# Plain loads and computed row numbers at the start of a Fourier mixing and hard-swish kernel

## The chip, the cores and the metric

The kernel runs on one core of a Trainium2 chip. The metric is device microseconds of one execution. Before the change the median of 3 runs is 1931.91 us (1931.62 to 1932.03).

The core has TensorE (PE, with its weight loads as PEld), VectorE (DVE), ScalarE (ACT), GpSimd (POOL) and SyncE (SP). DMAs are issued from SP, ACT and POOL and carried by 16 DMA engines. Each engine works through its own instructions in order and waits on semaphores.

## The reference

```python
# x: (8, 3008, 256) f32; w_in: (256, 2048); w_out: (2048, 256), given as 8-byte floats
X = np.fft.fft(x, axis=1)
X = np.fft.fft(X, axis=2).real          # mixing over sequence and features
h = X.reshape(24064, 256) @ w_in
out = (h * np.clip(h + 3.0, 0.0, 6.0) / 6.0) @ w_out
```

## The kernel before, in words

The Fourier transform over 3008 = 47 x 64 positions is done in two stages, stage 1 over 47 and stage 2 over 64, and symmetric halves of it are added ahead of the products ("folds"): a row group of x (64 + 48 partitions, 4 positions of 256 values in each) is added to its partner group, which lies mirrored in memory. The transform over the 256 features is multiplied into `w_in` once (`fold_w_in`), with a table `C`. Then come 24064 rows of an MLP in chunks: products `u` and `v` (L541), an activation on DVE and ACT, and the products with `w_out` (L616 and L636).

The batches are worked in four pairs. Only the start for the first batch is touched by the change; it is written out by hand, engine by engine, in the order of the program (`manual_schedule`).

- `load_half` fetches one group m of the first batch with two indirect DMAs from POOL: the forward rows and the partner rows (`gather`, L174). The row numbers stand in `IX`, cast by DVE (L875) from the table `FI` that SP loads first. Groups come in the order 3, 0, 1, 2 (`ORDER`).
- `fold_half` (L204 to L233) adds partners on DVE, `stage1_early` (L320 to L364) does the products on PE, copies them to `z` (L350 to L352) and stores `z` to memory (`zd`, L364). `load_g_half` (L432) reads it back, transposed, for stage 2 (`stage2_half`, L451; `spread_by_pe`, L472).
- The weights arrive as 8-byte floats, in 16 pieces of 512 KB (`load_w`, L740 and L744, POOL). A piece is turned into 4-byte floats by `exponent_a` (bytes, ACT, L760), `exponent_b` (PE, L774, with the matrix `E`), `exponent_c` (ACT, L777), `mantissa` (DVE, L785, L786) and `join` (DVE, L794, or L800 for `w_out`). A `w_in` piece is then multiplied by `C` (`fold_w_in`, PE, L829) and copied to `W1` (L832). The last row of each block of `W1` is wanted as a column `WN`: `send_wn` (L817) sends it by a small DMA from SP; for the first two blocks a small product (L946) makes it.
- `keep_awake` (L853) multiplies zeros on PE where there is nothing else to do.
- `see` (L903) is a small copy on POOL that holds back the loads behind it until its operand is there.

Piece 0 of `w_in` holds the column blocks f = 0 and 1, piece 1 the blocks 8 and 9. One MLP step with index fc uses the blocks fc and fc + 8. In the program's order both pieces are loaded ahead of all gathers, their exponents are done ahead of stage 1, and both are folded between stage 1 and stage 2:

```python
    for j in range(2):
        load_w(j)
    ...
    for k, m in enumerate(ORDER):
        load_half(hb, m)
```

A DMA takes one of 8 semaphore lanes for each kind of issuer; the ninth waits for the first to land.

Of the kernel before, what the change touches and what calls it, by code (L numbers as in the profile page):

```python
# [58 lines left out]
def kernel(  # L59
# [113 lines left out]
    def gather(xr, i, nr=PX, skip=0):  # L173
        nc.gpsimd.indirect_dma_start(  # L174
            out=xr[0:nr].rearrange("p n d -> p (n d)"), out_offset=None, in_=x_r,
            in_offset=bass.IndirectOffsetOnAxis(ap=IX[0:nr, i:i + 1], axis=0), element_offset=skip,
        )

    class Half:
# [6 lines left out]
    def take_half(hb, m, pool=xpool, tag="x"):  # L186
        hb.x[m], hb.xr[m] = x_tile(pool, tag), x_tile(pool, tag)

    def load_half(hb, m):
        start = hb.b * N1 * N2 * D  # L190
        gather(hb.x[m], NP * NXC + m, P, start + D)
        gather(hb.xr[m], m, P, start)

    def load_zero(o, hb, queue):
        queue.dma_start(out=o, in_=x_pn[hb.b * N1:(hb.b + 1) * N1, 0, :])

    def zero_slot(hb):
        return hb.x[NM - 1][PB:PB + N1, XC - 1, :]
# [332 lines left out]
    def mlp1_products(ch, fc, between=None):  # L531
        of, nq, q = ch.ck % 2 * TB, ch.nq, ch.pr.q[ch.ck // 2]
        u = ps_h.tile([P, 2, TB], F32, tag="uv", name="u")
        v = ps_h.tile([P, 2, TB], F32, tag="uv", name="v")
        for blk, ps in ((0, u), (1, v)):
            if blk and between:
                between()
            r = slice(0, P - blk)
            for i in range(2):
                f = fc + i * NF  # L540
                nc.tensor.matmul(ps[:, i, 0:nq], W1[r, blk, f * P:(f + 1) * P], q[r, blk, of:of + nq],  # L541
                                 start=True, stop=True)
        return u, v
# [182 lines left out]
    STRAIGHT = (0, 1, 8, 9, 14, 15)  # L726
    NEXT = {4: 10, 5: 11, 6: 12, 7: 13, 8: 14, 9: 15}

    def in_column(n, i):
        return (2 * n + i * NF) * P  # L730

    def load_w(j):
        kind, n, i = PIECES[j]

        pool, tag, bufs = (wpool, "st", 2) if j in STRAIGHT else (spool, "t", None) if j in (2, 3) else (xpool, "x", None)
        st = pool.tile([P, 2 * WB], I32, tag=tag, bufs=bufs, name="st")
        o = st[:].bitcast(moe_w_in.dtype)
        if kind == "in":
            cs = slice(in_column(n, i), in_column(n, i) + WB // 2)
            nc.gpsimd.dma_start(out=o.rearrange("p (c j) -> p c j", c=2),  # L740
                                in_=moe_w_in[:, cs].rearrange("(c p) f -> p c f", p=P))
# [11 lines left out]

    def exponent_a(j):
        top = raw[j][:].bitcast(I16).rearrange("p (n four) -> p n four", four=4)[:, :, 3]
        for i in range(2):
            low = PM[j % len(PM)][:, i].bitcast(U8).rearrange("p (n two) -> p n two", two=2)[:, :, 0]
            nc.scalar.activation(low, top, AF.Identity, bias=bias[:, i:i + 1], scale=(1 - 2 * i) / 16.0)  # L760

    def exponent_b(j, own=False):
        pm = [PM[j % len(PM)][:, i].bitcast(F16) for i in range(2)]
        if starting[0] and not own:
            exs[j] = ps_h.tile([P, WB], F32, tag="uv", name="ex")[:]
        elif own:
            exs[j] = ps_d.tile([P, WB], F32, tag="d", name="ex")[:]
        elif j % 2 == 0:
            exs[j] = bank([P, WB], "ex")[:]
        else:  # L770

            exs[j] = spare[1 if j % 4 == 1 else 0][:].rearrange("p i n -> p (i n)")
        for i in range(2):
            nc.tensor.matmul(exs[j], E[:, i], pm[i], start=(i == 0), stop=(i == 1))  # L774
# [41 lines left out]
    def send_wn(f):  # L816
        nc.sync.dma_start(out=WN[:, f:f + 1], in_=W1[P - 1:P, 1, f * P:(f + 1) * P])  # L817

    def fold_w_in(j):

        _, n, k = PIECES[j]
        nb = WB // 2
        cs = slice(in_column(n, k), in_column(n, k) + nb)
        wi = w.pop(PIECES[j]).rearrange("p (i f) -> p i f", i=2)

        ps = bank([P, 2, nb], "wps") if starting[0] else spare[k]
        for blk in range(2):
            for i in range(2):
                nc.tensor.matmul(ps[:, blk], C[:, i, blk * P:(blk + 1) * P], wi[:, i], start=(i == 0), stop=(i == 1))  # L829
        fs = range(cs.start // P, cs.stop // P)  # L830
        if starting[0]:
            nc.vector.tensor_copy(W1[:, :, cs], ps[:])  # L832
            return wi, fs
# [15 lines left out]
    def keep_awake(n, ps=None):  # L849
        if ps is None:  # L850
            ps = ps_d.tile([P, 2 * TB], F32, tag="d", name="awake")
        for i in range(n):
            nc.tensor.matmul(ps[:], ones[:], Z[:], start=True, stop=True)  # L853
# [1 line left out]
    Z = spool.tile([P, 2 * TB], F32, tag="s", name="Z")  # L855
    nc.vector.memset(Z[:], 0.0)
    nc.vector.memset(ones[:], 1.0)
    keep_awake(6)
    hb = halves[0]
    nc.sync.dma_start(out=FI[:], in_=c_stage1[:, 14 * PB:])  # L860
    nc.sync.dma_start(out=F[:], in_=c_stage1[:, 0:7 * PB])
    first_slot = qpool.tile([P, 2 * TB], F32, tag="qn", name="first_slot")
    load_zero(first_slot[PB:PB + N1, 0:D], hb, nc.sync)
# [6 lines left out]
    def clear_bytes(j):  # L870
        nc.vector.memset(PM[j][:].rearrange("p i n -> p (i n)").bitcast(I32), 0x64006400)

    clear_bytes(0)
    nc.vector.memset(half[:], 0.5)
    nc.vector.tensor_copy(IX[:], FI[:, 0:NIX])  # L875
    clear_bytes(1)
    clear_bytes(2)
    for k, m in enumerate(ORDER):
        take_half(hb, m, *((xpool, "x"), (xpool, "x"), (qpool, "q"), (apool, "a"))[k])

    def clear_table(b):
        r = slice((1 - b) * N2, (2 - b) * N2)
        t = T[r, b].rearrange("p g a k n -> p g (a k n)")
        nc.scalar.copy(t, Z[r].unsqueeze(1).to_broadcast([N2, NG, 2 * TB]))

    clear_table(0)

    def head(j):
        exponent_a(j)
# [13 lines left out]
        nc.gpsimd.tensor_copy(seen[:], x)  # L903

    for j in range(2):
        load_w(j)
    nc.gpsimd.affine_select(E[:, 0], ones[:], pattern=[[-1, P]], compare_op=AL.is_equal, fill=0.0, base=0,
                            channel_multiplier=1)  # L910
    nc.scalar.mul(E[:, 1], E[:, 0], -1.0)
# [6 lines left out]
    for j in range(2):  # L918
        exponent_a(j)
        mantissa(j)  # L920
    exponent_b(0)
    keep_awake(2)
    exponent_b(1, own=True)
    nc.scalar.copy(zero_slot(hb), first_slot[PB:PB + N1, 0:D])
    exponent_c(0)
    exponent_c(1)
    clear_table(1)
    keep_awake(4, bank([P, 2 * TB], "awake"))
# [12 lines left out]
    join(1)  # L941
    folds = [fold_w_in(j) for j in range(2)]
    wn = ps_d.tile([P, 2], F32, tag="d", name="wn")
    for c, (wi, fs) in enumerate(folds):
        for i in range(2):
            nc.tensor.matmul(wn[:, c:c + 1], wi[:, i, 0:P], C[:, i, D - 1:D], start=(i == 0), stop=(i == 1))  # L946
    nc.vector.tensor_copy(WN[:, 0:NFC:NF], wn[:])
    for wi, fs in folds:
        send_wn(fs[1])
# [7 lines left out]
    mantissa(2)  # L957
    exponent_a(2)
    exponent_b(2)
    mantissa(3)  # L960
    exponent_a(3)
    exponent_c(2)
# [197 lines left out]
def _tables(B, S, D):  # L1160
# [41 lines left out]
    f = np.concatenate([f0.reshape(128, -1), f1.reshape(128, -1), row.reshape(128, -1), forward, sign], axis=1)  # L1202

    k = k1[:, None] + N1 * np.arange(N2)
    n2 = np.arange(N2 // 2) + 1
# [42 lines left out]
```

## Time and profile before

| | |
|---|---|
| median of 3 runs | 1931.91 us |
| profiled execution | 1931.28 us, its span 1929.6 us |
| granted TensorE clock | 0.999 |
| PE busy | 1916.0 us, 99% |
| DVE, ACT, POOL busy | 1426.9, 679.6, 1443.3 us |
| bytes by DMA | 99.02 MB, 51 GB/s over the span |
| DMA rate in the first 32 us | 275 GB/s |

Times in the rows are in microseconds from the start of the span. A row of the timeline gives start, duration, engine (a name with q is the engine's DMA queue), line, operation, destination and source with their shapes, a count, and in brackets the idle time of the engine before it with what ended it. A row of busy times by stretch gives the stretch, its length, the busy time and the instruction count of each engine, the granted clock, the share of time that the DMA engines were busy, and GB/s.

### The profile page before, as it was taken

Reading aid. Unit: us, or ns where it says so; the run is one execution under the profiler, and the core shown is the slowest. Engines: PE = TensorE matmul, PEld = TensorE weight load, DVE = VectorE, ACT = ScalarE, POOL = GpSimd, SP = SyncE. Lnnn points to the kernel's source line nnn. Section 1 sums busy time; section 2 is a strip of 40 time slices with the busy share of each in tenths; the row PEclk is TensorE's granted clock in tenths of the full one; section 3 lists DMA queues with packets and bytes.
Section 4 is the critical chain, followed back from the end, with each engine's and each line's share of the span. In section 5 each row is a group of like instructions: output and inputs, shape, how many; then the busy total and the mean of one; then the engine's idle time right before and its main releaser. Section 6 shows DMA issues by size and latency. Waiting matters only on the chain.

```text
span 1929.6 us, 28216 instructions
## 1 busy us (share of the span) xinstructions
PE 1916.0 (99%) x9362; PEld 1652.4 (86%) x9362; DVE 1426.9 (74%) x2762; ACT 679.6 (35%) x1164; POOL 1443.3 (75%) x1652
## 2 busy tenths in 40 slices
PE   9999999999999999999999999999999999999998
PEld 5688888888988888888898888888899888888887
DVE  7867776777777777777787777777778777777777
ACT  6533333333333333333333333333333333333332
POOL 4697888896688778787678877878666667666765
PEclk9999999999999999999999999999999999999999
DMA  8432232211112222121111221221110101101000
GB/s 285 123 88 51 62 81 65 64 44 40 30 39 71 55 52 55 45 56 37 27 38 50 51 55 44 53 53 50 36 28 20 28 17 27 34 11 28 19 21 20
DMA packets 154473, 99.02 MB, mean 51 GB/s; under 512 B 121941, under 2 KB 135998, under 8 KB 154326
## 3 DMA queue, kind: packets, MB, share of 16 engines
q1 hardware_dynamic: 141926, 57.38, 12.3%
q0 software_dynamic: 11456, 39.56, 7.0%
q8 instruction: 74, 1.21, 0.3%
q14 instruction: 73, 0.60, 0.1%
q10 hardware_dynamic: 944, 0.26, 0.1%
HBM read 59.84 MB, written 37.32 MB: 50 GB/s over the span
## 4 chain that ended last, share of the span: by engine, by line
PE 96%; DVE 2%; ACT 1%; DMA 0%; issue 0%; SPq 0%; DVEq 0%; ACTq 0%; POOLq 0%
PE acc L636 56%; PE v L541 16%; PE u L541 16%; PE ps L490 2%; PE acc L616 1%; PE ps L279 1%; DVE a L592 1%; PE spare L829 1%; DVE s L550 1%; DVE o L697 0%; ACT t L589 0%; PE ps L451 0%; DMA st<-in_moe_w_in_dram 0%; PE awake L853 0%; DVE u L573 0%
## 5 line engine op out<-in xcount | busy, mean ns | idle before, releaser
L606 POOL TENSOR_TENSOR c<-a 128x512 f32<-128x512 f32 (+1 forms) x375 | 469.1, 1251 | 360.2 <-PE acc L636 309.6
L636 PE MATMUL acc<-c,G 128*128 128x256 f32 (+1 forms) x3008 | 697.2, 375 | 0.0
L589 ACT ACTIVATE t<-u,half 128x512 f32<-128x512 f32 (+1 forms) x384 | 260.6, 679 | 1142.6 <-DVE u L560 1063.3
L636 PEld LDWEIGHTS acc<-c,G 128*128 128x128 f32 x3008 | 565.2, 190 | 71.6 <-POOL c L606 0.4
L550 DVE SCALAR_TENSOR_TENSOR s<-qn,WN,u 128x256 f32<-128x256 f32 (+1 forms) x768 | 330.5, 472 | 341.0 <-PE u L541 338.1
L636 PE MATMUL acc<-a,G 128*128 128x256 f32 (+1 forms) x2256 | 541.6, 375 | 0.0
L636 PEld LDWEIGHTS acc<-a,G 128*128 128x128 f32 x2256 | 421.0, 189 | 73.6 <-issue 20.2
L541 PE MATMUL v<-q,W 127*128 127x256 f32 (+1 forms) x1536 | 389.3, 375 | 2.3 <-DVE a L592 2.3
L541 PE MATMUL u<-q,W 128*128 128x256 f32 (+1 forms) x1536 | 388.0, 375 | 0.2 <-ACT q L454 0.2
L592 DVE SCALAR_TENSOR_TENSOR a<-t,u 128x512 f32<-128x512 f32 (+2 forms) x448 | 264.1, 601 | 101.0 <-ACT t L589 97.3
L541 PEld LDWEIGHTS v<-q,W 127*128 127x128 f32 x1536 | 288.0, 190 | 42.9 <-DVE a L592 3.1
L541 PEld LDWEIGHTS u<-q,W 128*128 128x128 f32 x1536 | 285.8, 190 | 37.4 <-issue 2.4
L606 POOL TENSOR_TENSOR c<-a,c 128x256 f32<-128x256 f32 (+1 forms) x375 | 268.6, 716 | 29.4
L606 POOL TENSOR_TENSOR c<-c,a 128x256 f32<-128x256 f32 (+1 forms) x375 | 268.3, 716 | 29.4
L560 DVE TENSOR_TENSOR u<-s,v 128x512 f32<-128x512 f32 x352 | 245.0, 696 | 37.4 <-DVE s L550 0.9
L592 DVE SCALAR_TENSOR_TENSOR a<-t,v 128x512 f32<-128x512 f32 (+1 forms) x480 | 263.6, 565 | 0.3
L589 ACT ACTIVATE t<-v,half 128x512 f32<-128x512 f32 (+1 forms) x384 | 260.5, 678 | 0.6 <-issue 0.4
L562 DVE TENSOR_TENSOR v<-v,s 128x512 f32<-128x512 f32 x352 | 243.9, 693 | 0.0
L606 POOL TENSOR_TENSOR r<-w,e 128x256 f32<-128x256 f32 (+1 forms) x92 | 88.7, 985 | 3.6
L646 ACT ACTIVATE e<-acc 128x512 f32<-128x512 f32 (+2 forms) x184 | 83.3, 544 | 0.0
L697 DVE STREAM_TRANSPOSE o<-r 128x256 f32<-128x256 f32 (+1 forms) x192 | 72.5, 415 | 0.2
L606 POOL TENSOR_TENSOR w<-w,e 128x512 f32<-128x512 f32 (+1 forms) x46 | 57.5, 1251 | 3.6
(139 smaller groups left out, 775.9 us busy)
## 6 DMA issues: line engine op xcount, KB each, us to landing
out_dram<-o SPq DMA_DIRECT2D x744, 32.0 KB
g<-zd SPq DMA_DIRECT2D x42, 256.0 KB
zd<-z SPq DMA_DIRECT2D x48, 192.0 KB
xt<-in_x_dram POOLq DMA_DIRECT2D x21, 256.0 KB
st<-in_moe_w_in_dram POOLq DMA_DIRECT2D x8, 512.0 KB
st<-in_moe_w_out_dram POOLq DMA_DIRECT2D x8, 512.0 KB
qn<-qd SPq DMA_DIRECT2D x16, 256.0 KB
xt<-in_x_dram POOLq DMA_DIRECT2D x17, 192.0 KB
```

The costliest lines, as they stand in the source:

```text
L279: nc.tensor.matmul(ps[b][h * PB:(h + 1) * PB, 0:n], F[rows(b), 0:PB], y[rows(b), 2 * h:2 * h + n], start=True, stop=not last, skip_group_c ...
L490: nc.tensor.matmul(ps[:, blk, u * P:n].rearrange("p (b k) -> p b k", b=2), g[:, kk, blk * (P + 1):blk * (P + 1) + P], T[:, :, gr, blk, kk, ...
L541: nc.tensor.matmul(ps[:, i, 0:nq], W1[r, blk, f * P:(f + 1) * P], q[r, blk, of:of + nq], start=True, stop=True)
L550: nc.vector.scalar_tensor_tensor(s[:, i, 0:nq], qn[:, of:of + nq], WN[:, f:f + 1], u[:, i, 0:nq], op0=AL.mult, op1=AL.add)
L560: nc.vector.tensor_tensor(u[:], s[:], v[:], op=AL.add)
L562: nc.vector.tensor_tensor(v[:], v[:], s[:], op=AL.subtract)
L589: nc.scalar.activation(t, h, AF.Relu, bias=half[:], scale=scale)
L592: nc.vector.scalar_tensor_tensor(dst, t, 1.0, h, op0=AL.min, op1=AL.mult)
L606: (eng or nc.gpsimd).tensor_tensor(out, in0, in1, op=AL.add)
L636: nc.tensor.matmul(ch.acc[i // 2][:, i % 2, 0:ch.n], G[:, i, fc, :], mv, start=(fc == 0 and i % 2 == 0), stop=(fc == NF - 1), skip_group_c ...
L646: nc.scalar.mul(ch.e[:, k:i + 1, 0:ch.n], ch.acc[i // 2][:, 0:i + 1 - k, 0:ch.n], 1.0 / WS)
L697: nc.vector.transpose(o[:, 0:n // DH, h], ch.r[:, m, h, 0:n].rearrange("p (j i) -> p j i", i=DH))
```

## The change

Row numbers are made on POOL by two iotas and a maximum, into a new table `IT`; the table of the other groups is stored as integers in `FI` and used without a cast. The forward rows of the first batch come by plain loads: the first half of the first group from ACT's queue, everything else from SP's, the zero column directly to its place (48 rows in place of 47). Only partners are gathered, 112 rows in place of 128. The first weight piece is loaded ahead of the last gather, the second behind it; the first two pieces hold other columns than before: piece 0 the blocks 0 and 8, piece 1 the blocks 1 and 9, each loaded by two DMAs of 128 columns. Preparation of piece 0 moves between the groups of stage 1, that of piece 1 behind stage 1, interleaved with pieces 2 and 3; `WN` of the first two pieces comes by `send_wn`. Two PSUM tiles at the first steps change pools, and wake-up products become fewer.

```diff
-    IX = consts.tile([P, NIX], I32, name="IX")
+    IX = FI[:, 0:NIX].bitcast(I32)
+    IT = consts.tile([P, NM], I32, name="IT")
...
+    def load_rows(hb, m, h, queue):
+        c, nr = m + h * NM, (PB, N1 + 1)[h]
+        n = XC - (c == NXC - 1)
+        queue.dma_start(out=hb.x[m][h * PB:h * PB + nr, 0:n, :], in_=x_pn[0:nr, c * XC + 1:c * XC + 1 + n, :])
...
-        v = ps_h.tile([P, 2, TB], F32, tag="uv", name="v")
+        pool, tag = (ps_d, "d") if ch.first and fc == 1 else (ps_h, "uv")
+        v = pool.tile([P, 2, TB], F32, tag=tag, name="v")
...
+    def in_columns(n, i):
+        if n == 0:
+            return [(i + h * NF) * P for h in range(2)]
+        return [(2 * n + i * NF + h) * P for h in range(2)]
...
-    keep_awake(6)
+    keep_awake(7)
...
+    for h in range(2):
+        nc.gpsimd.iota(IT[h * PB:(h + 1) * PB], [[-1, NM]], base=2 * NXC * N1 - 1 - h * NM,
+                       channel_multiplier=-2 * NXC)
+    nc.gpsimd.tensor_single_scalar(IT[:], IT[:], 0, op=AL.max)
+    load_rows(hb, ORDER[0], 0, nc.scalar)
+    load_rows(hb, ORDER[0], 1, nc.sync)
+    load_zero(zero_slot(hb), hb, nc.sync)
+    for m in ORDER[1:]:
+        for h in range(2):
+            load_rows(hb, m, h, nc.sync)
+        if m == ORDER[1]:
+            nc.sync.dma_start(out=F[:], in_=c_stage1[:, 0:7 * PB])
     nc.sync.dma_start(out=FI[:], in_=c_stage1[:, 14 * PB:])
-    nc.sync.dma_start(out=F[:], in_=c_stage1[:, 0:7 * PB])
...
-    for j in range(2):
-        load_w(j)
...
     for k, m in enumerate(ORDER):
-        load_half(hb, m)
+        if k == NM - 1:
+            load_w(0)
+        gather(hb.xr[m], m)
...
+    load_w(1)
     nc.gpsimd.dma_start(out=C[:], in_=c_dim.rearrange("(h p) d -> p h d", p=P))
...
     for k, m in enumerate(ORDER):
         if m in SPLIT:
+            mantissa(0)
             for j in range(2):
                 fold_columns(hb, m, j, nc.vector)
             join(0)
...
         stage1_early(hb, m)
+        if k == 0:
+            exponent_a(0)
+        elif k == 2:
+            exponent_b(0)
+            exponent_c(0)
...
+    mantissa(1)
+    fold_w_in(0)
+    exponent_a(1)
+    exponent_b(1)
+    keep_awake(1)
+    exponent_a(2, (0,))
+    exponent_c(1)
+    exponent_a(2, (1,))
+    mantissa(2)
     join(1)
-    folds = [fold_w_in(j) for j in range(2)]
...
-    see(W1[:, 0, NF * P:NF * P + 1])
+    see(w[PIECES[1]][:, 0:1])
...
     exponent_b(2)
+    exponent_a(3, (0,))
+    exponent_c(2)
+    exponent_a(3, (1,))
     mantissa(3)
...
+    fold_w_in(1)
     exponent_b(3)
-    keep_awake(1)
     join(2)
     tail(3)
     stage2_half(hb, 0)
```

More of the change, by code (lines that the diff above doesn't have):

```diff
@@ L738, in load_w @@
         if kind == "in":
-            cs = slice(in_column(n, i), in_column(n, i) + WB // 2)
-            nc.gpsimd.dma_start(out=o.rearrange("p (c j) -> p c j", c=2),
-                                in_=moe_w_in[:, cs].rearrange("(c p) f -> p c f", p=P))
+            c0, c1 = in_columns(n, i)
+            for h, cs in enumerate((slice(c0, c1 + P),) if n else (slice(c0, c0 + P), slice(c1, c1 + P))):
+                nf = cs.stop - cs.start
+                nc.gpsimd.dma_start(out=o.rearrange("p (c j) -> p c j", c=2)[:, :, h * P:h * P + nf],
+                                    in_=moe_w_in[:, cs].rearrange("(c p) f -> p c f", p=P))
         else:
@@ L746, in load_w, with exponent_a @@
         raw[j] = st
-    def exponent_a(j):
+    def exponent_a(j, signs=range(2)):
         top = raw[j][:].bitcast(I16).rearrange("p (n four) -> p n four", four=4)[:, :, 3]
-        for i in range(2):
+        for i in signs:
             low = PM[j % len(PM)][:, i].bitcast(U8).rearrange("p (n two) -> p n two", two=2)[:, :, 0]
@@ L763, in exponent_b @@
         pm = [PM[j % len(PM)][:, i].bitcast(F16) for i in range(2)]
-        if starting[0] and not own:
+        if (starting[0] or j == 4) and not own:
             exs[j] = ps_h.tile([P, WB], F32, tag="uv", name="ex")[:]
@@ L829, in fold_w_in @@
                 nc.tensor.matmul(ps[:, blk], C[:, i, blk * P:(blk + 1) * P], wi[:, i], start=(i == 0), stop=(i == 1))
[L830 to L833, printed above, removed]
+        fs = (c0 // P, c1 // P)
+        if n == 0:
+            o = W1[:].rearrange("p b (h f) -> p b h f", h=2)[:, :, :, c0:c0 + P]
+            nc.vector.tensor_copy(o, ps[:].rearrange("p b (h f) -> p b h f", h=2))
+            for f in fs:
+                send_wn(f)
+            return
         nc.scalar.copy(W1[:, :, cs], ps[:])
@@ L871, in clear_bytes @@
         nc.vector.memset(PM[j][:].rearrange("p i n -> p (i n)").bitcast(I32), 0x64006400)
-    clear_bytes(0)
     nc.vector.memset(half[:], 0.5)
[L875 to L879, printed above, removed]
+    for j in range(3):
+        clear_bytes(j)
     def clear_table(b):
@@ L917 @@
         load_w(j)
[L918 to L926, printed above, removed]
+    clear_table(0)
+    nc.scalar.mul(E[:, 1], E[:, 0], -1.0)
     clear_table(1)
-    keep_awake(4, bank([P, 2 * TB], "awake"))
     for k, m in enumerate(ORDER):
         if m in SPLIT:
+            mantissa(0)
             for j in range(2):
@@ L1201, in _tables @@
     sign = 1.0 - 2.0 * (np.arange(128)[:, None] % 2)
-    f = np.concatenate([f0.reshape(128, -1), f1.reshape(128, -1), row.reshape(128, -1), forward, sign], axis=1)
+    index = np.concatenate([row.reshape(128, -1), forward], axis=1).astype(np.int32).view(np.float32)
+    f = np.concatenate([f0.reshape(128, -1), f1.reshape(128, -1), index, sign], axis=1)
     k = k1[:, None] + N1 * np.arange(N2)
```

33 lines of the change are left out of this document (10 added, 23 removed).

## The prediction, as recorded before the run

> **What bounds the kernel now.** I read the page first, then busy time by stretch, then the first 45 us instruction by instruction, then the chain that ended last over the same stretch.
>
> ```profile
> PE 1916.0 (99%) x9362; PEld 1652.4 (86%) x9362; DVE 1426.9 (74%) x2762; ACT 679.6 (35%) x1164; POOL 1443.3 (75%) x1652
> ```
> ```profile
> 0.00:32.00 32.00, 29.15 (x239) 17.87 (x240) 20.56 (x53) 20.65 (x34) 17.81 (x28) 1.00 0.84 275
> 32.00:110.00 78.00, 76.44 (x302) 50.20 (x301) 66.22 (x121) 44.80 (x76) 46.03 (x61) 1.00 0.52 160
> 110.00:300.00 190.00, 190.00 (x912) 162.80 (x911) 135.67 (x244) 67.95 (x118) 159.54 (x179) 1.00 0.27 66
> ```
>
> The columns of the second fence are the stretch, its length, busy time of PE, PEld, DVE, ACT and POOL, the granted clock, the DMA share and GB/s. PE is full from 110 us on (190.00 of 190.00). Both kernels issue the same instructions in the same order from the first MLP chunks on, so whatever the change does is a shift of the point at which PE becomes continuously busy. The chain shows where that is:
>
> ```profile
> 32.24 0.95 DVE s L550 x2
> ...
> 40.40 0.60 DVE wi L794
> 41.04 1.99 PE spare L829 x8
> ```
>
> From 41.04 on the chain is PE work almost without a break. From 32.24 to 41.04 it is DVE work in a row, in an order that the change leaves as it is. So the question is when the first `s` on DVE starts: 32.24 now. The start before it, in order of time (start, duration, engine, line, operation, idle before):
>
> ```profile
> 0.41 0.12 POOL L1232 MEMSET const-uint8-127<- 128x1 uint8 x1
> 0.82 0.41 SPq L860 DMA_DIRECT2D FI<-in_c_stage_dram  x1
> 1.29 0.42 SPq L861 DMA_DIRECT2D F<-in_c_stage_dram  x1
> 1.37 1.67 POOL L740 DMA_DIRECT2D st<-in_moe_w_in_dram  x2 [0.84 <-POOLq L1232]
> 1.68 6.89 PE L853 MATMUL awake<-Z,ones 128*128 128x512 f32 x12 [1.68 <-DVE ones L857]
> 2.11 2.75 ACT L884 COPY T<-Z 64x3072 f32<-64x3072 f32 x1
> 2.76 0.29 DVE L875 CAST IX<-FI 128x36 int32<-128x36 f32 x1 [0.57 <-DMA FI<-in_c_stage_dram]
> 3.14 0.30 POOL L909 TENSOR_SCALAR_AFFINE_SELECT E<-ones 128x128 f16<-128x128 f32 x1
> 3.64 1.07 POOL L174 DMA_INDIRECT xt<-in_x_dram,IX  x1 [0.19 <-DVE PM L871]
> 5.02 0.97 POOL L174 DMA_INDIRECT xt<-in_x_dram,IX  x1 [0.31 <-issue]
> 7.82 0.43 DVE L785 TENSOR_SCALAR top<-st 128x512 int32<-128x512 int32 x1 [3.81 <-DMA st<-in_moe_w_in_dram]
> 8.29 0.69 DVE L786 SCALAR_TENSOR_TENSOR top<-st,top 128x512 f32<-128x512 uint32 x1
> 11.66 0.56 DVE L215 TENSOR_TENSOR xt<-xt 111x381 f32<-111x381 f32 x1 [1.48 <-DMA xt<-in_x_dram,IX]
> 12.57 0.94 POOL L174 DMA_INDIRECT xt<-in_x_dram,IX  x1 [0.30 <-issue]
> 15.43 0.69 DVE L215 TENSOR_TENSOR xt<-xt 111x508 f32<-111x508 f32 x1
> 16.77 0.69 DVE L215 TENSOR_TENSOR xt<-xt 111x508 f32<-111x508 f32 x1
> 19.30 0.17 DVE L226 TENSOR_TENSOR y<-xt 111x8 f32<-111x8 f32 x1
> 20.21 1.57 DVE L204 TENSOR_TENSOR xt<-xt 111x4 f32<-111x4 f32 x6 [0.74 <-DMA xt<-in_x_dram,IX]
> 21.70 0.68 DVE L794 TENSOR_TENSOR wi<-top,ex 128x512 f32<-128x512 f32 x1
> 22.87 3.72 PE L829 MATMUL wps<-wi,C 128*128 128x256 f32 x16
> 23.02 0.69 DVE L352 COPY z<-ps 112x512 f32<-112x512 f32 x1 [0.65 <-PE ps L344]
> 23.79 0.67 ACTq L364 DMA_DIRECT2D zd<-z  x1
> 24.51 2.73 ACT L760 ACTIVATE PM<-st,bias 128x512 uint8<-128x512 int16 x4 [0.95 <-DVE wi L794]
> 24.90 0.69 DVE L832 COPY W<-wps 128x512 f32<-128x512 f32 x1 [0.59 <-PE wps L829]
> 26.23 0.92 SPq L432 DMA_DIRECT2D g<-zd  x2
> 27.24 1.02 PE L774 MATMUL ex<-PM,E 128*128 128x512 f16 x4
> 27.39 0.18 POOL L903 COPY seen<-W 128x1 f32<-128x1 f32 x1 [10.54 <-DVE W L832]
> 27.86 1.07 ACT L777 ACTIVATE ex<-ex 128x512 int32<-128x512 f32 x2 [0.62 <-PE ex L774]
> 29.18 1.13 PE L451 MATMUL ps<-T,g 128*128 128x128 f32 x8
> ```
> ```profile
> 2.00:4.00 2.00, 2.00 (x3) 0.85 (x3) 1.37 (x5) 1.99 (x2) 1.71 (x4) 1.00 0.77 188
> 4.00:6.00 2.00, 2.00 (x5) 0.88 (x4) 0.01 (x1) 1.17 (x2) 1.68 (x2) 1.00 0.96 341
> 10.00:12.00 2.00, 1.94 (x7) 0.72 (x6) 0.52 (x2) 1.51 (x3) 1.60 (x2) 1.00 1.02 412
> ```
>
> DVE waits 1.48 us for the first two gathers and cannot fold before 11.66. Once it folds it stops only once, 0.74 us at 20.21, for the last pair. The DMA engines are full from 4 us on (share 0.96 and over, 341 to 412 GB/s), and both weight pieces, 2 x 512 KB, stand ahead of the gathers. So the start is bounded by bytes ahead of the first fold, then by DVE's folds, then by a DMA round trip: z copied at 23.71, g read from 26.23, stage 2 on PE at 29.18, `s` at 32.24.
>
> **The first fold.** Removed ahead of it: the load of FI, the cast and the wait for both (the gather could not start before the cast's end at 3.05), and the two weight pieces (1.67 us of POOL, 1 MB). Added on POOL: two iotas of 64x4 and a maximum of 128x4. No row here shows an iota; the three together lie between one affine select (0.30) and three times the longest POOL row of the start, the 1.07 of a gather (3.2 us). I take 0.9, three affine selects, the nearest operation on the same engine. POOL can begin at about 1.0 (between the 0.53 us after which it idles and the 1.37 at which it first issues), so the first gather is issued from 1.9 to 3.0 instead of 3.64.
>
> The forward rows go by SP and ACT from 0.82 on, at 0.41 us an issue: one load on ACT's queue, on SP the other part of the first group, the zero column (48 rows), two loads, F, two loads, two loads, FI. The last three wait for a lane, that is for the first loads to land, and nobody needs them before 15 us. First group and zero column are 448 KB; bytes of FI were there by 2.76, 1.9 us after its issue, so these start near 2 and are down near 4.5 at 350 GB/s. When the first partner gather (112 x 4 KB, 448 KB) starts to move at about 3.4, some 1.1 MB of other forward rows and F is queued beside it. With half of 400 GB/s it takes 2.3 us, with all of it 1.1, behind all of the others 4.6; I add 0.7 for landing. So the first fold starts at 5.2, 6.4 or 8.7; with the upper bound of the row numbers each of these is 2.3 later, 11.0 at the latest. I take 6.5, equal shares, as the nearest rows only show engines that are full and not who gets them. Gain 11.66 - 6.5 = 5.2 us.
>
> **Folds to the end of stage 1.** Folds run as before: 3.77 for the first group (11.66 to 15.43), 1.34 for the second, 2.70 for the third (16.77 to 19.47). Then the first piece's mantissa, 1.16 (7.82 to 8.98), formerly in the shadow of the gathers' wait, now lies between the third and the last group. The 0.74 wait goes if the last gather lands by 6.5 + 8.97 = 15.5. Ahead of it are 2.0 MB of forward rows, F and FI, 1.34 MB of gathers, 0.5 MB of weights, and itself 0.45: 4.3 MB from 2 us on at 350 to 400 GB/s is 13 to 14.5, plus landing. That just fits. Net +0.4. ACT now does the exponent bytes of piece 0 (half of 2.73) between the z copies of the first and second group; the second group's copies move by about 1.0 and end 0.6 before the last group needs their banks: nothing.
>
> E's second half, the two clearings of T (2.75 each, ACT busy to about 9) and PM's clearing stay ahead of the first z copies, beside the loads: nothing; with a first fold 3 us earlier still a clearing would stand in the z copies' way, at up to 2.75. PE: one wake-up matmul more (1.15, by the mean of the 6.89 for six) carries it to about 9.7; the first stage 1 matmul comes at 6.5 + 3.8 = 10.3.
>
> **Stage 1 to the first `s`.** Now only piece 0 (columns of f = 0 and 8) is needed for the first chunk, but piece 1 is still folded ahead of stage 2 in PE's order, and its steps hang on each other. I count from the end of the last fold, D (before 21.78). As before: last z copies end at D+1.95, ACT's store issue until D+2.7. ACT then: bytes of piece 1 (1.37) to D+4.1, half of piece 2 to 4.8, exponent of piece 1 (0.55) to 5.35; DVE joins piece 1 (0.68) to D+6.1; PE folds piece 1 (half of 3.72) behind the second half of piece 2's exponents, D+6.5 to D+8.35; piece 3's exponents follow (half of 1.02): stage 2 starts at D+8.8. Before it started at D+7.4 (29.18), because both pieces had their exponents done ahead of stage 1. From stage 2 to `s` is 3.06 as before. So +1.4. DVE's list up to there (two mantissas of 1.16 more, one copy the less) ends at D+10.5, before `s` at D+11.9: covered. The g round trip ends at D+7.4; weight pieces 2 and 3 are still moving when the last z is stored, which may cost it up to 1.2 us: covered by the 8.8, not more.
>
> The bound of that term is 0 below (stage 2 goes when g is there, D+7.4, if PE and ACT overlap better than I count) and 2.6 above (another 1.2 for the same contention).
>
> WN of f = 0 and 8 now comes by two small DMAs behind the g loads on SP instead of a copy on DVE: issued near D+5.5, against `s` at D+11.9. Hidden. POOL's `see` waits for piece 1's join (D+6.1) instead of the second copy (27.39, D+5.6): the next loads go 0.5 later against D, before a use that comes 1.4 later. v of the second chunk moves to another bank, so PE need not wait for a gate; DVE is full there, so nothing.
>
> **Sum.** -5.2 + 0.4 + 1.4 = -3.4 us. The profiled execution took 1931.28 (span 1929.6), 0.6 below the median of 1931.91; taken from the median it gives 1928.5.
>
> **A rule against it.** The 4 to 6 us row shows the DMA engines 96% busy with what POOL's queue and SP's give them. The Trainium skill, DMA: Bandwidth & Descriptors, section "Rules for kernel authors", says that spreading DMAs over SP, ACT and GpSimd for bandwidth doesn't help, since all run on the same 16 engines and interleave. By that rule only bytes and issue time would be gained, which is the second rival.
>
> **Rivals.**
> - More gain. The first gather gets through at 5.5 to 6 and the chain behind stage 1 costs 0 to 0.6 instead of 1.4. For it: the g loads alone set 29.18 about as late as the wake-up matmuls ahead of it do, so PE's order may have had slack. Against: ACT's chain above is counted from its own rows. -5.9 + 0.4 + 0.6 = -4.9: 1927.0.
> - Bytes are bytes. Forward rows, queued first, pass ahead of the gathers, and the first fold starts at 8.7 to 9.5, or the last gather lands 2 to 3 us after 15.5. For it: 4.3 MB must pass anyway, and weight rows cut to 128 columns make smaller packets. With the fold at 9.1: -2.6 + 0.4 + 1.4 = -0.8: 1931.1.
> - Slower. The row numbers on POOL are dear: everything behind them, four gathers, four weight loads, C and T, waits. The sum is zero when the first fold starts at 9.9, that is when the first gather is issued from 5.3 on, a step of 4.3 us; at 6 us it is +1.7: 1933.6. For it: no iota in the trace. Against: no short POOL operation in the trace is over 0.3 us.
>
> **Numbers.** The forecast (fold at 6 to 8, -1.9 to -3.8) has 0.42, more gain 0.36, bytes 0.14, dear row numbers 0.08. 0.2% is 3.9 us, about what a measurement can tell: faster takes the 0.36; the forecast, the bytes and 0.03 of the last are within, 0.59; slower 0.05. The range goes from 1926.6 (a fold at 5.5, nothing lost behind D) to 1931.5, and leaves out a tail of the first rival and most of the last.
>
> **What would show it.** First fold on DVE near 6.5, with its wait on the gather and not on the rows; last fold without a wait near 15.5; stage 2 on PE near D+8.8 with PE's wait on ACT's bytes of piece 2 or 3, not on g; first `s` near 28.9; PE full from about 37.7. Wrong if the first gather starts after 3 us, if the last fold waits over 1 us, or if PE's rows behind 110 us change their length.

## The result and the profile after

The changed kernel takes 1939.72 us (median of 6, 1937.51 to 1941.32) where the kernel before takes 1931.97 on the same chip: a ratio of 1.0040, with a 95% interval of 1.0027 to 1.0053. It is 0.4% slower, 7.75 us. The forecast of 1928.5 and the whole range were wrong, and so was the direction. The profiled execution is the fastest of the six: 1937.51 us, its span 1935.8, so the trace explains 6.2 us of the 7.75; what the other 1.5 us are, no trace shows.

Busy times by stretch of the kernel after (stretch, length, PE, PEld, DVE, ACT, POOL, granted clock, DMA share, GB/s):

```profile
0.00:32.00 32.00, 26.80 (x193) 16.02 (x194) 16.07 (x43) 16.03 (x27) 11.36 (x21) 0.73 0.82 221
110.00:300.00 190.00, 190.00 (x915) 162.06 (x914) 137.08 (x246) 67.29 (x115) 159.77 (x178) 1.00 0.27 68
```

Behind 110 us nothing changed (190.00 of 190.00, as before). In the first 32 us two numbers fell that the prediction took for granted: the granted clock from 1.00 to 0.73, and the DMA rate from 275 to 221 GB/s. The timeline of the kernel after, by the prediction's stations:

```profile
0.91 0.30 POOL L878 IOTA IT<- 64x4 int32 x2 [0.40 <-POOLq L1249]
1.31 0.24 POOL L880 TENSOR_SCALAR IT<-IT 128x4 int32<-128x4 int32 x1
1.66 8.23 PE L868 MATMUL awake<-Z,ones 128*128 128x512 f32 x14 [1.66 <-DVE ones L872]
1.85 1.15 POOL L175 DMA_INDIRECT xt<-in_x_dram,IT  x1 [0.30 <-POOL IT L880]
8.91 0.56 DVE L221 TENSOR_TENSOR xt<-xt 111x381 f32<-111x381 f32 x1 [5.66 <-DMA xt<-in_x_dram,IT]
11.78 0.34 PE L326 MATMUL pt<-y,F 47*64 47x2 f32 x8 [1.89 <-DVE y L234]
15.96 0.69 DVE L221 TENSOR_TENSOR xt<-xt 111x508 f32<-111x508 f32 x1 [2.09 <-DMA xt<-in_x_dram,IT]
19.04 1.41 ACT L771 ACTIVATE PM<-st,bias 128x512 uint8<-128x512 int16 x2 [2.65 <-DMA st<-in_moe_w_in_dram]
20.55 0.44 PE L326 MATMUL pt<-y,F 47*64 47x2 f32 x8 [1.16 <-ACT z L356]
20.60 1.57 DVE L210 TENSOR_TENSOR xt<-xt 111x4 f32<-111x4 f32 x6 [0.42 <-DMA xt<-in_x_dram,IT]
27.89 0.69 DVE L358 COPY z<-ps 112x512 f32<-112x512 f32 x1 [2.78 <-PE ps L350]
35.30 1.05 PE L457 MATMUL ps<-T,g 128*128 128x128 f32 x8
38.67 0.87 DVE L557 SCALAR_TENSOR_TENSOR s<-qn,WN,u 128x256 f32<-128x256 f32 x2 [1.59 <-issue]
```

The first `s` starts at 38.67 instead of 32.24, 6.43 later: that is the slowdown (6.2 us between the two profiled executions). By stations, against the rows of before:

| station | before | after | the shift grows by |
|---|---|---|---|
| first fold | 11.66 | 8.91 | -2.75 |
| last fold ends | 21.78 | 22.17 | +3.14 |
| last z copy ends | 23.71 | 28.58 | +4.48 |
| stage 2 starts | 29.18 | 35.30 | +1.25 |
| first `s` | 32.24 | 38.67 | +0.31 |

So 2.75 us were won at the first fold and lost again over the other three groups: waits of 2.09 for the third group's rows, 0.37 for the weight piece and 0.42 for the last gather, and the mantissa of piece 0 between them. The largest loss lies between the last fold and the last z copy, where before needed 1.93 us and after 6.41. The chain that ended last shows what stood in the way there (kernel after, start, length, what):

```profile
6.52 12.41 DMA st<-in_moe_w_in_dram
...
19.04 1.41 ACT PM L771 x2
20.45 0.11 ACT z L356 x2
20.56 0.43 PE pt L326 x8
```

The first weight piece was 12.41 us on its way. ACT waited for it (2.65 us at 19.04) with the z copies of the second group queued behind it, and PE's third group waited for those (1.16 at 20.55). And PE worked at half its clock (kernel after, then the same stretch before):

```profile
10.00:11.00 1.00, 0.00 (x0) 0.00 (x0) 0.97 (x4) 0.00 (x0) 0.77 (x2) 1.00 1.03 229
12.00:13.00 1.00, 0.60 (x15) 0.52 (x13) 0.97 (x5) 0.16 (x1) 0.47 (x1) 0.73 1.04 225
13.00:14.00 1.00, 1.00 (x10) 0.60 (x5) 0.87 (x3) 0.16 (x1) 0.08 (x1) 0.50 1.02 242
26.00:28.00 2.00, 2.00 (x33) 1.68 (x33) 0.11 (x1) 0.37 (x3) 0.00 (x0) 0.50 0.40 145
29.00:30.00 1.00, 1.00 (x5) 0.80 (x4) 0.65 (x1) 0.57 (x1) 0.00 (x0) 0.74 0.13 33
```
```profile
12.00:13.00 1.00, 1.00 (x4) 0.52 (x3) 1.00 (x4) 0.81 (x2) 0.70 (x2) 1.00 1.02 414
13.00:14.00 1.00, 1.00 (x3) 0.39 (x3) 0.90 (x3) 1.00 (x1) 0.99 (x2) 1.00 1.04 418
```

PE stood idle from 9.89 (end of the wake-ups) to 11.78. From about 12.5 to 29.5 the clock was 0.50 (in the rows with 0.73 and 0.74 it changed about halfway). Before, at 12 to 14 us PE was busy with wake-up products alone, and those are what the change took away. The third view is the DMA queues over 10 to 14 us, before and then after (packets, MB, share of 16 engines' time; q0 is POOL's queue, q1 SP's):

```profile
DMA packets 454, 1.65 MB, mean 414 GB/s; under 512 B 50, under 2 KB 50, under 8 KB 454
q0 software_dynamic: 454, 1.65, 102.5%
```
```profile
DMA packets 279, 0.93 MB, mean 234 GB/s; under 512 B 51, under 2 KB 51, under 8 KB 279
q0 software_dynamic: 137, 0.48, 53.6%
q1 hardware_dynamic: 142, 0.45, 50.2%
```

The two queues did get equal shares, but of 234 GB/s, not of 400. The engines are as busy as before and the packets as large; each takes longer. Share x 16 engines x 4 us / packets is 0.14 us a packet before, and 0.25 and 0.23 on the two queues after.

### The profile page after: what moved, and what is told of

It is laid out like the page before. It is cut to its first block, busy times and chain, and to the rows that moved or that the text cites. A ratio compares the mean times of both kernels' runs of the same rounds, so it can differ in the third digit from the quotient of the medians.

```text
span 1935.8 us, 28201 instructions
## 1 busy us (share of the span) xinstructions
PE 1919.1 (99%) x9344; PEld 1656.6 (86%) x9344; DVE 1426.4 (74%) x2760; ACT 679.1 (35%) x1163; POOL 1441.6 (74%) x1653
## 4 chain that ended last, share of the span: by engine, by line
PE 95%; DVE 2%; DMA 1%; ACT 1%; issue 0%; POOL 0%; SPq 0%; ACTq 0%; DVEq 0%; POOLq 0%
PE acc L643 56%; PE v L548 16%; PE u L548 16%; PE ps L496 2%; PE acc L623 1%; PE ps L285 1%; DMA st<-in_moe_w_in_dram 1%; DVE a L599 1%; PE spare L841 1%; DVE s L557 0%; DVE o L704 0%; ACT t L596 0%; PE ps L457 0%; DVE u L580 0%; DMA out_dram<-o 0%
```

## The experiments

My theory after this: two causes, the clock and the DMA rate, beside the +1.4 us of the new order behind stage 1 that was foreseen. Against it stood: one of the two is only a consequence (late data make the idle time), or weight pieces cut to 128 columns are the slow transfers.

**The clock.** e1_warm is the changed kernel with two more wake-ups at the start and five behind the second group. e2_before_gap is the kernel before without the six between weights and stage 1.

```diff
-    keep_awake(7)
+    keep_awake(9)
...
+        elif k == 1:
+            keep_awake(5)
```
```diff
     exponent_b(0)
-    keep_awake(2)
...
-    keep_awake(4, bank([P, 2 * TB], "awake"))
```

> The changed kernel with two more wake-up products ahead of stage 1 and five between the second and the third row group, so that PE has no gap; nothing else moves. Clock theory (the loss is the half clock granted from 12.5 to 29.5 us): granted clock 1.00 in every stretch, and the products behind 20.5 us shrink by half (third group 2.2 to 1.2, exponents 1.0 to 0.4, last group 4.1 to 2.1, first fold of w_in 2.9 to 1.8): some 4.6 us back or more, 1935 or less. Data theory (late rows and weights are the loss): the bytes of piece 0 still wait on ACT until about 19, the first fold still starts near 8.9, and 3 us or more of the loss against the kernel before stay: 1935 or more. If the clock alone were the cause: 1931 or less.

> The kernel before without the two and the four wake-up products ahead of stage 1, so that PE has a gap of some 4 us in front of stage 1; its loads are as they were. Clock theory: the granted clock falls to 0.50 in a stretch of stage 1, the products there take twice as long, and the time rises by 3 to 6 us: 1935 to 1938. Data theory: these products do no work that counts, the order of loads is unchanged, 1931.9 within 1.

e1_warm: 1935.78 us, ratio 1.0023 (1.0013 to 1.0033); the clock is 1.00 all through, `s` comes at 36.08. Its last fold and its last z copy:

```profile
21.27 1.57 DVE L210 TENSOR_TENSOR xt<-xt 111x4 f32<-111x4 f32 x6 [0.22 <-DMA xt<-in_x_dram,IT]
25.49 0.69 DVE L358 COPY z<-ps 112x512 f32<-112x512 f32 x1 [0.43 <-PE ps L350]
```

From the end of the fold (22.84) to the end of the copy (26.18) it takes 3.34 us, against 6.41 in the changed kernel and 1.93 in the kernel before. e2_before_gap: 1938.25, 1.0031 (1.0019 to 1.0042). Its rows by stretch:

```profile
13.00:14.00 1.00, 0.00 (x0) 0.00 (x0) 0.90 (x3) 1.00 (x1) 1.00 (x2) 0.50 1.00 381
14.00:15.00 1.00, 0.12 (x4) 0.13 (x7) 0.97 (x5) 1.00 (x1) 1.00 (x2) 0.50 1.05 401
```

Loads run at 381 and 401 GB/s (418 and 401 before) and its last fold starts at 20.51 (20.21 before), but at clock 0.50 the last z copy starts at 28.36 instead of 23.02. Products of zeros that nobody reads are thus worth 6.3 us in the kernel before. In the changed kernel their lack costs 3.9 by the medians; the rest, 3.8, is something else, and in e1_warm the data are as late as in the changed kernel (third group's fold at 17.08, with a wait of 2.27).

**Which transfers are slow.** Four kernels change the shape of the two kinds of x transfers. e3_rows128 fetches the forward rows of groups 2 to 4 by one plain load of 128 consecutive rows (other rows than the reference's, so the time is that of the transfer's shape alone). f1_gather128 gathers partners with 128 rows instead of 112. e4_gather_rows gathers the forward rows too, 112 rows, their numbers by iotas. f3_all128 is e4_gather_rows with 128 rows in both gathers.

```diff
 e3_rows128
+    def load_wide(hb, m, queue):
+        queue.dma_start(out=hb.x[m][:], in_=x_pn[0:P, m * XC + 1:m * XC + 1 + XC, :])
...
-        for h in range(2):
-            load_rows(hb, m, h, nc.sync)
+        load_wide(hb, m, nc.sync)
 f1_gather128
-        gather(hb.xr[m], m)
+        gather(hb.xr[m], m, P)
 e4_gather_rows (f3_all128: all of tile and table instead of 0:PX, and gather(hb.xr[m], m, P))
-        for h in range(2):
-            load_rows(hb, m, h, nc.sync)
...
+        if k > 0:
+            gather_rows(hb.x[m], IT[0:PX, 1, m:m + 1], D)
         gather(hb.xr[m], m)
```

> The changed kernel, but the forward rows of the second, third and fourth group come by one plain load of 128 consecutive rows each (512 KB, all partitions) in place of two loads of 64 and 48 rows; the upper partitions so hold other rows than they should, and the output is that of wrong rows. More bytes than before (1.54 MB in place of 1.34), same queue, same mixture with POOL's gathers. If loads of half the partitions are what makes the DMA engines slow (about 240 GB/s from 4 to 18 us, at a share of 1.0): the rate goes to 350 to 400, the first three groups stop waiting, W piece 0 lands near 15, and the time falls by 3 us or more, to 1936 or less. If it is the mixture of a plain queue with the gathers': the rate stays near 240 and the time near 1939.7 or above.

> The changed kernel, but the forward rows of the second, third and fourth group come by gathers again (112 rows each, their numbers by two iotas more, 0.3 us), only the first group by plain loads. Data theory, either form: 350 to 400 GB/s from 5 us on, first fold at 6.5 to 7.5, no wait of 2 us at the third group, W piece 0 by 15; PE's gap ahead of stage 1 closes, so the clock stays up as well; 1929 to 1931. Clock theory alone: the gap of PE in front of stage 1 depends on the first fold; if that stays near 8.9 the clock falls again and the time stays at 1937 to 1940.

> The changed kernel, but each partner gather takes 128 rows instead of 112 (the last 16 are not used), 0.26 MB more. If a gather of 112 rows is what keeps the DMA engines at about 240 GB/s: the rate between 6 and 18 us rises to 320 or more although bytes are added, the first fold starts at 8 or earlier, the third group's wait of 2.1 us shrinks below 1, W piece 0 lands before 17, and the time falls to 1934 to 1937, more if the clock stays up. If not: rate, waits and time as in the changed kernel, or 0.5 to 1 us worse for the bytes.

> The changed kernel, but the forward rows of the second to fourth group are gathered, and all gathers take 128 rows; the first group's forward rows stay plain loads. Against the earlier run with 112-row gathers only the row count differs. If 112 rows is the slow form: 380 to 410 GB/s from 6 us on, as in the kernel before; no wait of 2 us at the third group; last gather by 15.5 to 16.5; 1929 to 1933 if the clock stays up, some 4 more if it falls. If the row count does not matter: 240 to 260 GB/s and 1935 again.

| kernel | forward rows | partner rows | GB/s at 8 to 12 us | us | ratio, interval |
|---|---|---|---|---|---|
| after | plain, 64 + 48 | gather 112 | 265 | 1939.72 | 1.0040 (1.0027 to 1.0053) |
| e3_rows128 | plain, 128 | gather 112 | 302 | 1938.4 | 1.0034 (1.0022 to 1.0045) |
| f1_gather128 | plain, 64 + 48 | gather 128 | 295 | 1937.6 | 1.0030 (1.0018 to 1.0041) |
| e4_gather_rows | gather 112 | gather 112 | 246 | 1935.45 | 1.0014 (1.0005 to 1.0024) |
| f3_all128 | gather 128 | gather 128 | 366 | 1933.96 | 1.0009 (0.9999 to 1.0019) |

The rates, of after, e3, f1, e4 and f3 in turn, are read from these rows:

```profile
8.00:12.00 4.00, 2.11 (x13) 0.79 (x11) 3.02 (x9) 0.44 (x1) 2.77 (x4) 1.00 1.07 265
```
```profile
8.00:12.00 4.00, 1.37 (x4) 0.30 (x2) 1.94 (x5) 0.44 (x1) 2.79 (x4) 0.93 1.04 302
```
```profile
8.00:12.00 4.00, 2.10 (x11) 0.71 (x11) 2.95 (x9) 0.44 (x1) 2.88 (x4) 1.00 1.05 295
```
```profile
8.00:12.00 4.00, 2.76 (x21) 1.21 (x23) 3.76 (x13) 1.08 (x2) 3.39 (x5) 1.00 1.04 246
```
```profile
8.00:12.00 4.00, 3.89 (x32) 2.16 (x31) 3.90 (x14) 1.51 (x4) 3.38 (x5) 1.00 1.01 366
```

Most of what was expected of these runs did not come. e4_gather_rows was to reach 350 to 400 GB/s if the plain loads were what is slow, and stayed at 246. f1_gather128 was to reach 320 or more, with the first fold at 8 and piece 0 before 17; the fold came at 8.99, the third group waited 2.45 us and piece 0 reached ACT at 18.88. e3_rows128 came between its two cases (350 to 400 GB/s and 1936 us or less, or 240 and 1939.7). Nor do the times follow the rates: e4_gather_rows, with the lowest rate, is 4.3 us faster than the changed kernel. Its first fold is at 7.96, ACT has piece 0 at 16.88 instead of 19.04, and the last z copy ends at 26.44 instead of 28.58.

The cleanest pair is the last, which differs in the number of gathered rows alone. Over 10 to 14 us only POOL's queue moves, e4_gather_rows first, then f3_all128:

```profile
q0 software_dynamic: 273, 0.98, 103.1%
```
```profile
q0 software_dynamic: 437, 1.54, 100.8%
```

The same queue, the same busy share, and 0.24 against 0.15 us a packet: 245 against 384 GB/s. A gather of 112 rows is slower than one of 128, which carries 14% more bytes. (The times of the two runs are 1.5 us apart, and their intervals overlap.) The plain loads to 64 and 48 partitions are the other half of it: at 8 to 12 us, with one of the two kinds made wide, the rate rises to about 300; with 128-row gathers in place of both, to 366. At 10 to 14 us the changed kernel has 234 GB/s, e3_rows128 291 and f1_gather128 only 254, and there f1_gather128's 128-row gathers, beside narrow plain loads, take 0.24 us a packet too:

```profile
q0 software_dynamic: 148, 0.54, 55.0%
```

So the price of a shape depended on what moved beside it. The Trainium skill, SBUF — State Buffer, section "Door 1: The DMA port swizzle", says that the rate of a transfer depends on how many of 16 ports its partitions reach, and in the section "Can I just issue two DMAs to hit both halves?" that two transfers to the two halves don't add up to a whole one. For the plain loads the rows agree in direction (265 to 302 when they are made whole). For 112 partitions the page gives no price, and why they cost as much as they do here no run shows.

In all four the clock still fell, each time behind a pause of PE. In f3_all128 it did so although the first fold came at 6.98 and the wake-ups met stage 1 without a gap. The pause came later:

```profile
16.58 0.30 PE L332 MATMUL pt<-y,F 47*64 47x2 f32 x5 [2.35 <-ACT z L362]
```

The third group's fold had waited 1.68 us for its data there, and the z copies stood behind the bytes of piece 0, which began at 15.07. So the rate alone is not the whole loss. e3_rows128 and f1_gather128 tell the rate, but little of the time: both ran stage 1 at half clock.

**Wider weight pieces.** f2_wide_w is the changed kernel with the old columns of pieces 0 and 1, one DMA of 256 columns each. f4_all128_wide_warm has this, 128-row gathers, and wake-ups of 8 and 1.

```diff
-        if n == 0:
-            return [(i + h * NF) * P for h in range(2)]
...
-            for h, cs in enumerate((slice(c0, c1 + P),) if n else (slice(c0, c0 + P), slice(c1, c1 + P))):
+            for h, cs in enumerate((slice(c0, c1 + P),)):
```

> The changed kernel with the old columns in the first two weight pieces: each one DMA of 256 columns (rows of 2 KB) instead of two of 128 columns (rows of 1 KB); order and place unchanged. If the short rows are a cause: piece 0 lands 1 us or more before the 18.95 of the changed kernel, ACT's bytes of piece 0 follow, and the time falls by 1 to 2 us. If the queue ahead of it is the cause: piece 0 lands within 0.5 us of 18.95 and the time stays within 1 us of 1939.7.

> All that the theory of both causes asks for in one kernel: the former with the old weight columns (one DMA of 256 columns each), one more wake-up product ahead of stage 1 and one between the second and the third group. If late data and the clock are the whole loss: clock 1.00 throughout, first fold near 7, first s at 29 to 31, 1928.5 to 1931. If the new order behind stage 1 costs more than 1.4 us by itself: 1931 to 1934 with the clock at 1.00.

f2_wide_w: 1942.51 us, 1.0059 (1.0042 to 1.0075), the slowest of all. Piece 0 reached ACT at 20.24, later than the changed kernel's 19.04 and outside both cases expected; the first fold is at 9.92. That the narrow pieces are the slow transfers is so not borne out. It also shows what the new choice of columns is for. With the old one, the second half of the first `s` needs a row of piece 1, and waits for it (f2_wide_w, DVE):

```profile
39.39 0.48 DVE L557 SCALAR_TENSOR_TENSOR s<-qn,WN,u 128x256 f32<-128x256 f32 x1 [1.19 <-issue]
41.94 0.48 DVE L557 SCALAR_TENSOR_TENSOR s<-qn,WN,u 128x256 f32<-128x256 f32 x1 [2.06 <-DMA WN<-W]
```

f4_all128_wide_warm: 1935.44, 1.0018 (1.0008 to 1.0028), above both ranges expected, although its last fold starts at 17.72, 2.5 before the kernel before's. Where that gain went (PE, then one row of its clock):

```profile
30.78 1.80 PE L463 MATMUL ps<-T,g 128*128 128x128 f32 x8 [2.34 <-DMA g<-zd]
```
```profile
32.00:33.00 1.00, 1.00 (x6) 1.00 (x6) 0.00 (x0) 0.38 (x1) 0.97 (x1) 0.50 1.08 357
```

The last z copy ended at 21.46, but z's trip through memory took 9.3 us from there, beside weight pieces that were still loading and the next loads that POOL had released. The pause of 2.34 us then cost the clock again.

**Both causes mended.** g1_all128_warm is f3_all128 with 8 wake-ups at the start, 4 behind the second group, 2 ahead of stage 2, and the bytes of piece 0 behind the z copies they had blocked. h1_all128_fit has the bytes there too, and 8 wake-ups, then 2 and 2, and 1. In both, plain loads are left for the first group alone; the others are gathered again. g2_before_iota is the kernel before with the row numbers by iotas and nothing else.

```diff
 g1_all128_warm, on f3_all128
-        if k == 0:
-            exponent_a(0)
+        if k == 1:
+            exponent_a(0)
+            keep_awake(4)
 h1_all128_fit, on f3_all128
+            keep_awake(2)
         elif k == 2:
             exponent_b(0)
             exponent_c(0)
+            keep_awake(2)
 g2_before_iota, on the kernel before
+        nc.gpsimd.iota(IT[h * PB:(h + 1) * PB, 0], [[-1, NM]], base=2 * NXC * N1 - 1 - h * NM,
+                       channel_multiplier=-2 * NXC)
+        nc.gpsimd.iota(IT[h * PB:(h + 1) * PB, 1], [[1, NM]], base=h * NM, channel_multiplier=2 * NXC)
```

> The changed kernel with 128-row gathers throughout (as f3_all128), wake-ups of 8 and 4 where PE waits, one more ahead of stage 2, and the bytes of piece 0 behind the second group's z copies instead of ahead of them. If the loss is the clock and the rate of the gathers, and nothing else: granted clock 1.00 from 5 us on, last z copy near 22.8 (f3_all128 24.58 less about 1.8), stage 2 6.7 later at 29.5, first s at 32.6, where the kernel before has 32.24: 1932.3, ratio 1.000. If the trip of z through memory becomes the bound when the data come earlier (as in f4_all128_wide_warm): stage 2 at 30.5 to 31, PE waiting for g there, 1933.5 to 1934.5, ratio 1.001.

> g1_all128_warm with its wake-ups cut to what fits: in g1 four of them held PE from 15.45 to 19.08, while the third group's folds were there at about 16.8. Here two behind the second group and two behind the exponents of piece 0, and one instead of two ahead of stage 2. If the last 1.7 us against the kernel before (s at 33.95 and 32.24) are those wake-ups: last z copy ends at 22.5 to 22.9 instead of 23.74, stage 2 at 29.3 to 29.7 and s at 32.5, 1931.5, ratio 1.000. If the trip of z through memory is the bound by now, stage 2 stays at 30 or later with PE waiting for g, and 1932.3 to 1932.8. If two are too few for the clock, it falls to 0.50 after 17 us, and 1933.5 or more.

> The kernel before with the row numbers of the first batch made by iotas on POOL, all else as it was: this part of the change alone. If the start is bounded by bytes: POOL issues the first gather some 0.4 earlier (3.2 instead of 3.64), the first fold stays within 0.5 of 11.66 and s within 0.5 of 32.24; 1931.5 to 1932.2, ratio 1.000. If the wait for the table of row numbers held the start: the first fold 0.5 or more earlier and s with it, 1931.2. If iotas on POOL are dear, later by what they take.

g1_all128_warm: 1932.51, 1.0005 (0.9996 to 1.0014). h1_all128_fit: 1932.06, 1.0001 (0.9992 to 1.0010). The clock is 1.00 in both, and no loss is left that can be measured. In g1_all128_warm the last z copy ends at 23.74 and stage 2 starts at 30.57, as late as the second case expected, but PE doesn't wait for g there, and the time is nearer to the first. h1_all128_fit:

```profile
18.75 1.57 DVE L216 TENSOR_TENSOR xt<-xt 111x4 f32<-111x4 f32 x6 [1.33 <-DMA xt<-in_x_dram,IT]
22.83 0.69 DVE L364 COPY z<-ps 112x512 f32<-112x512 f32 x1 [1.91 <-PE ps L356]
33.37 0.87 DVE L563 SCALAR_TENSOR_TENSOR s<-qn,WN,u 128x256 f32<-128x256 f32 x2 [1.59 <-PE u L554]
```

The last fold starts 1.46 earlier than before, and `s` 1.13 later. Of these 2.59 us, 1.27 go between the last fold's end (20.32) and the last z copy's (23.52): 3.20 us where the kernel before needs 1.93, since the last two wake-ups held PE until the last group's first product at 20.53. Stage 2, at 30.00, comes 6.48 behind the copy where before it was 5.47: 1.01, the new order behind stage 1. The other 0.31 lie between stage 2 and `s`. The z copy came later than the 22.5 to 22.9 expected, and stage 2 at the edge of what the second theory expects, though without a wait for g. Neither version beats the kernel before. What the clock and the place of the bytes are worth one by one on f3_all128, and what h1_all128_fit does without its last two wake-ups, was not tried.

g2_before_iota: 1932.11, 1.0003 (0.9994 to 1.0012), first fold at 11.35 and `s` at 32.82, 0.58 later, just outside the 0.5 expected. The first gather is issued at 3.91, not 0.4 earlier as expected but 0.27 later, so an earlier gather is not what this run tries. The row numbers alone are worth nothing that can be measured.

## Why the prediction was wrong

The sum failed on the path from the first fold to the last z copies. It put -5.2 and +0.4 there and nothing between the last fold and the last z copies; measured were -2.75, +3.14 and +4.48, so the last z copies came 4.87 later instead of 4.8 earlier. It took over a DMA rate for transfers of another shape, let ACT wait for a weight piece at no cost, and had no term for the clock.

- **Row numbers (right).** Two iotas and the maximum end at about 1.55; the first gather is issued at 1.85, where I took 1.9. The rival with dear row numbers falls.
- **First fold (mis-sized).** The term was -5.2, with "half of 400 GB/s" for the gather. Half was about right (44.1% for POOL's queue at 4 to 8 us, while the first gather was on its way, and 53.6% at 10 to 14), 400 was not. It was 246 GB/s at 4 to 8 us, and 234 later:

```profile
DMA packets 336, 0.98 MB, mean 246 GB/s; under 512 B 45, under 2 KB 135, under 8 KB 336
```

  The fold came at 8.91 and the term was -2.75. The 400 was read from rows in which 128-row gathers and full-width pieces moved, and taken over for transfers of other shapes. The change narrowed both kinds, and I counted only their bytes.
- **Folds to the end of stage 1 (failed).** "The 0.74 wait goes if the last gather lands by 15.5 [...] That just fits." The last gather landed at 20.6, behind a wait of 0.42; the third group's fold alone waited 2.09. +3.14 instead of +0.4. This is the second rival's "last gather lands 2 to 3 us late", and 5 came of it, by rate and not by order of arrival.
- **ACT's bytes between the z copies (failed).** I costed them "nothing". That held only if the weight piece was there; it came at about 18.93 (6.52 + 12.41), and the z copies behind it waited with it.
- **The clock (left out).** I worked out that wake-ups end at 9.7 and the first product comes at 10.3 (measured 9.89 and 11.78), and that the six products between weights and stage 1 go, but gave neither a price. The profile before had no idle stretch in which it could be read; e2_before_gap gives it, 6.3 us in the kernel before, and e1_warm 3.9 (medians) in the changed one. The end of z's last copies, expected at D+1.95 as before (D is the end of the last fold), came at D+6.41; in e1_warm, at full clock, at D+3.34. So about 3.1 of the 4.5 us are the clock. The rest is a third group that starts late even then (21.52 in e1_warm), behind ACT's bytes of piece 0 and the wake-ups. The clock is the one error for which the sum had no term at all, and no rival contained it: the slower one was built on an instruction's price.
- **Stage 1 to `s` (right).** I put stage 2 at 6.85 behind the end of the last z copies (D+8.8 less D+1.95); it was 6.72. The term was +1.4, measured +1.25, and 0.31 more up to `s`. From stage 2 to `s` it is 3.37 us here and in h1_all128_fit (3.06 before); why, no run shows.
- **Hidden things.** `WN` by small DMAs stayed hidden, and PE's rows behind 110 us kept their length, as said.
- **The signs of being wrong.** None of the three named came: the first gather was issued at 1.85, the last fold waited 0.42, and the rows behind 110 us kept their length. None of them looked at PE's clock or at the third group.
- **Slips of arithmetic.** The lower end of the range, a fold at 5.5 with nothing lost behind D, is 1926.2 by the sum's own terms (-6.2 + 0.4), not 1926.6. 448 KB from 2 us on at 350 GB/s are down at 3.3, not 4.5. Nothing else rests on either.

Two additions bring the 7.75 us back: wake-ups take 3.9 off (to 1935.78), 128-row gathers with the bytes moved another 3.7 (to 1932.06). The intervals allow 2.5 us either way for the changed kernel and under 2 for the two others, so this split is rough. That both causes take part rests on the clock and the rates in the traces; that together, with the place of the bytes, they are the whole, on h1_all128_fit, which gives up most of the plain loads.

## What to carry to other kernels

Products that compute nothing may hold the clock: before taking one away, write down what PE does in that stretch without it, and price a fall to half clock over all PE work until it recovers. A DMA rate belongs to the shape it was measured with; where transfers were made narrower than 128 partitions here, the bytes saved were not time saved. And work moved into an in-order engine's queue beside critical copies makes its input a critical input.

## What was not expected of the hardware

- 112-row gathers moved 245 GB/s where 128-row gathers moved 384, with the DMA engines at 103 and 101% busy: a full DMA share does not tell the rate.
- The clock fell soon. In the kernel after, a pause of 1.89 us was followed by 0.73 in the row of 12 to 13 us. In e3_rows128 PE stood idle from 9.37 on, and the clock fell at about 11.4, 2.0 us into the pause:

```profile
11.00:12.00 1.00, 0.00 (x0) 0.00 (x0) 0.97 (x4) 0.00 (x0) 0.01 (x1) 0.70 1.05 311
```

  In e4_gather_rows two short pauses among tiny products were all that came before it:

```profile
10.82 0.34 PE L332 MATMUL pt<-y,F 47*64 47x2 f32 x8 [0.78 <-DVE y L240]
11.62 0.21 PE L335 MATMUL pt<-y,F 47*64 47x1 f32 x1 [0.46 <-DVE y L245]
```
```profile
12.00:13.00 1.00, 1.00 (x15) 0.83 (x8) 1.00 (x3) 0.39 (x2) 1.00 (x1) 0.88 1.02 242
13.00:14.00 1.00, 1.00 (x19) 1.00 (x22) 0.12 (x2) 0.49 (x2) 1.00 (x2) 0.50 1.04 250
```

  On the other hand h1_all128_fit had pauses of 0.50 and 0.28 us behind stage 1 with no fall. The Trainium skill, TensorE: Matmul & The Clock Gate, Part 1, gives about 3.4 us as the idle window after which the clock halves, and as long a busy one to bring it back. The first doesn't agree with these pauses: in none of them had PE been idle for more than 2.0 us when the clock fell.
- It came back late. In the kernel after, PE was busy without a pause from 13 to 18 us, and the clock stayed at 0.50 until about 29.5:

```profile
14.00:15.00 1.00, 1.00 (x16) 1.00 (x12) 0.00 (x0) 0.43 (x1) 0.00 (x0) 0.50 1.08 242
17.00:18.00 1.00, 1.00 (x16) 0.91 (x12) 0.97 (x3) 0.00 (x0) 0.00 (x0) 0.50 1.00 242
```

  Small products of stage 1, on 47 rows and 64 columns of the array, fill that stretch. Perhaps not every row that shows PE busy counts as activity for the clock. But the same products held a clock of 1.00 in the kernel before, from 15.49 on:

```profile
16.00:17.00 1.00, 1.00 (x22) 0.83 (x15) 1.00 (x4) 0.39 (x3) 0.85 (x2) 1.00 1.04 422
```

  Which measure decides, these runs don't settle.
